# DeltaNet attention followed by a hierarchical gated mixture of experts: large element-wise work on VectorE instead of GpSimd, routing pushed at every third round, scatters declared independent, one Sqrt for the norms

## The chip, the cores and the metric

The kernel runs on one core of one Trainium2 chip. Its time is the device time of one execution in microseconds (us); the profile is one such execution taken by the hardware profiler. The engines are PE (TensorE matmul; PEld is its weight load), DVE (VectorE), ACT (ScalarE), POOL (GpSimd) and SP (SyncE, which here only issues DMAs). Each takes its own instructions strictly in order.

## The reference

Two stages follow each other. The first is a delta-rule recurrence over 768 tokens for 4 batches and 8 heads of width 48; the second sends each of the 3072 resulting rows (384 wide) to one of 16 experts.

```python
k_n = k / (np.linalg.norm(k, axis=-1, keepdims=True) + 1e-06)
for t in range(S):
    y[:, :, t] = einsum('bhd,bhde->bhe', q[:, :, t], state)
    v_old = einsum('bhde,bhd->bhe', state, k_n[:, :, t])
    state = state + beta_t * einsum('bhd,bhe->bhde', k_n[:, :, t], v[:, :, t] - v_old)
...
x = y.transpose(0, 2, 1, 3).reshape(B * S, H * D)
g_idx = argmax(x @ w_group); e_idx = argmax(x @ w_expert[g_idx])      # per token
out[token] = g_w * e_w * (relu(x @ w1[g, e]) @ w2[g, e])              # softmax weights of the two picks
```

## The kernel before

**Attention.** The 768 tokens are cut into NCH = 24 chunks of C = 32; the 4 batches fill the 128 partitions. Four chunks make a group (RG = 4), six groups in all. For a chunk u:

- `gram(u)` multiplies keys by keys and queries into the PSUM tile `g_ps` (one buffer, tag "g", which `t_ps`, `l_ps` and `r_ps` share). ScalarE copies the key half into `gt`, then the query half into `gq`; GpSimd masks `gq` (L173). Grams run LEAD = 9 chunks ahead.
- `inverse(g)` inverts the 32x32 triangular matrices of a group's 1024 (chunk, batch, head) problems. It is a generator, one or a few instructions a step: a transposition (L185), norms by Ln and Exp on ScalarE (L192, L193), the product `m`·`r` (L214) and the matrix `cs` (L216), each 128x1024, then 30 pairs of VectorE instructions (L224 multiply, L228 add, j = 1 to 30, 30 to 240 elements), the product with `cs` (L230), the diagonal (L231) and a transposition to `mt` (L235). Outside group 0, L214 and L230 run on GpSimd; L216 and L231 do always.
- `scale(u)` multiplies the values by the norms into `vh` on GpSimd (L241).
- `advance(u)` is the recurrence: PE `a_ps` from the state, VectorE `f` = `vh` - `a_ps` (L260), PE `w_ps` from `mt` and `f`, ScalarE `w`, PE `s_ps`, ScalarE state `s_bd` (two instructions, L290), and so to `a_ps` of the next chunk. PE `o_ps` gives the chunk's output, ScalarE copies it into `x` (ten buffers).

**Routing.** `logits(u)` transposes `x` on PE (`t_ps`), multiplies by the router weights (`l_ps`), and VectorE copies the result to `lg`. `route(r)` is a generator of some 28 small steps for a group of four chunks, mostly VectorE, with `pick`, `hot` and four `acc` on GpSimd, one matmul pair `r_ps` that counts tokens ahead of each token, `rk`, `slot`, `slot_i` on VectorE, and then four times a small copy (L410) and an indirect DMA (L413) from GpSimd that scatters 128 rows of `x` to the experts' places in `x_dram`. The scatters all write `x_dram`, which is first filled with zeros by 16 DMAs from SP (L495).

**Order.** Everything but SP's queue is issued in the order in which the Python code runs. The list `behind` holds the running generators; `work(n)` goes n rounds over it and pushes each one step, `route` only at every second round. `work` stands between the steps of `advance`, so VectorE's queue holds 19 rounds of inverse and route steps per chunk between one `f` and the next. A generator that yields ACT_STEP or PE_STEP is held until `allow`, once a chunk. SP's queue is put in order by the framework, by its own estimate.

**Experts.** After the last scatter SP reads the sorted rows (`xg`, L523) and 16 experts run one after the other (L538 to L557).

Of the kernel before, what the change touches and what calls it, by code (L numbers as in the profile page):

```python
# [52 lines left out]
def deltanet_then_moe(  # L53
# [57 lines left out]
    with ExitStack() as first:  # L111
# [35 lines left out]
        zero = ap_.tile([128, STATIC * XW], F32, name="zero")  # L147
        nc.gpsimd.memset(zero, 0.0)

        gts, gqs, mts, norm, vhs, xs = {}, {}, {}, {}, {}, {}  # L150

        def gram(u):


            g, uu = divmod(u, RG)
            kqt = kqt_[u % NB]
            if uu == 0:
                gts[g] = wk.tile([128, C, RG, H], F32, tag="gt", name=f"gt{g}")
            g_ps = ps.tile([128, 2, 512], F32, tag="g", name=f"g_ps{u}")
            g_out = g_ps[:, :, 0:NP * 2 * C].rearrange("p f (j a t) -> p f j a t", j=NP, a=2)  # L160
            for j in range(NP):
                for b in range(B):
                    for hh in range(2):
                        rows = slice(hh * 64, hh * 64 + D)
                        nc.tensor.matmul(g_out[quads[b], hh, j], lhsT=kqt[rows, 0, j, quads[b]],  # L165
                                         rhs=kqt[rows, :, j, quads[b]], start=True, stop=True,
                                         skip_group_check=True)
            nc.scalar.activation(
                gts[g][:, :, uu].rearrange("p t (f j) -> p f j t", f=2), g_out[:, :, :, 0, :],
                ACT.Copy)  # L170
            gq = wk.tile([128, 2, NP, C], F32, tag="gq", name=f"gq{u}", bufs=LEAD + 1)
            nc.scalar.activation(gq, g_out[:, :, :, 1, :], ACT.Copy)  # L172
            nc.gpsimd.tensor_tensor(  # L173
                gq, gq, cut["upper"][:, None, None, :].to_broadcast([128, 2, NP, C]),
                op=ALU.mult)
            gqs[u] = gq

        def inverse(g):

            eng = nc.gpsimd if g else nc.vector
            m = wk.tile([128, C, C], F32, tag="m", name=f"m{g}")
            flat = m.rearrange("p i j -> p (i j)")
            nc.vector.transpose(out=flat, in_=gts.pop(g).rearrange("p t u h -> p (t u h)"))  # L185
# [3 lines left out]
                           for n in ("nrm", "r0", "r1")]  # L189
            nc.vector.tensor_tensor(r0, diag, cut["tiny"].to_broadcast([128, C]), op=ALU.max)  # L190
            yield ACT_STEP
            nc.scalar.activation(r0, r0, ACT.Ln)  # L192
            nc.scalar.activation(r0, r0, ACT.Exp, scale=0.5)  # L193
            yield
            nc.vector.reciprocal(r1, r0)
            yield
# [14 lines left out]
            yield  # L211
            norm[g] = sm.tile([128, C], F32, tag="normt", name=f"normt{g}")
            nc.vector.transpose(out=norm[g], in_=nrm)
            eng.tensor_tensor(m, m, r0[:, :, None].to_broadcast([128, C, C]), op=ALU.mult)  # L214
            cs = wk.tile([128, C, C], F32, tag="cs", name=f"cs{g}")
            nc.gpsimd.tensor_tensor(cs, cut["below"].rearrange("p (i j) -> p i j", i=C),  # L216
                                    r0[:, None, :].to_broadcast([128, C, C]), op=ALU.mult)
            for _ in range(6 if g else 0):
                yield
            for j in range(1, C - 1):  # L220
                n = C - 1 - j
                t = wk.tile([128, C * C // 4], F32, tag="t", name=f"t{g}_{j}")
# [4 lines left out]
                yield  # L227
                nc.vector.tensor_tensor(m[:, j + 1:, 0:j], m[:, j + 1:, 0:j], tv, op=ALU.add)  # L228
                yield
            eng.tensor_tensor(m, m, cs, op=ALU.mult)  # L230
            nc.gpsimd.tensor_scalar(diag, r0, -1.0, None, op0=ALU.mult)  # L231
            for _ in range(6 if g else 0):
                yield
            mt = wk.tile([128, RG * H, C], F32, tag="mt", name=f"mt{g}")
            nc.vector.transpose(out=mt.rearrange("p r i -> p i r"), in_=flat)  # L235
            mts[g] = mt
# [1 line left out]
        def scale(u):  # L238
            g, uu = divmod(u, RG)
            vh = wk.tile([128, H, D], F32, tag="vh", name=f"vh{u}")  # L240
            nc.gpsimd.tensor_tensor(  # L241
                vh.rearrange("p (j f) d -> p f j d", f=2),
                kv_[u % NV][:, 1].rearrange("p (j f) d -> p f j d", f=2),
                norm[g][:, uu * H:(uu + 1) * H].rearrange("p (f j) -> p f j", f=2)[:, :, :, None]
                .to_broadcast([128, 2, NP, D]), op=ALU.mult)
            vhs[u] = vh
# [90 lines left out]
            yield  # L337
            return den

        lg_ = {}  # L340

        def logits(u):

# [17 lines left out]
        def route(r):  # L361
# [46 lines left out]
            for g, u in enumerate(us):  # L408
                x = xs.pop(u)
                nc.gpsimd.tensor_copy(x[:, DM:DM + 1], cw[:, g])  # L410
                for _ in range(2):
                    yield
                nc.gpsimd.indirect_dma_start(  # L413
                    out=x_dram.rearrange("t p d -> (t p) d"),
                    out_offset=bass.IndirectOffsetOnAxis(ap=slot_i[:, g], axis=0),
                    in_=x[:, :], in_offset=None)
                yield


# [11 lines left out]
        def work(n):  # L431

            for _ in range(n):
                rounds[0] += 1
                for task, pace in [(t, 2 if t.__name__ == "route" else 1) for t in behind]:
                    if held.get(task) is None and rounds[0] % pace == 0:
                        push(task)

# [9 lines left out]

        with tc.manual_schedule(engines={mybir.EngineType.PE, mybir.EngineType.DVE,
                                         mybir.EngineType.Activation, mybir.EngineType.Pool}):  # L450
            for u in range(RG):
                gram(u)
            behind.append(inverse(0))
            for step in range(LEAD - RG):
                work(2)
                allow(ACT_STEP)
                gram(RG + step)
            while behind:
                work(1)
            scale(0)  # L460
# [4 lines left out]
            for u in range(NCH + 1):  # L465
# [3 lines left out]
                next(turned)  # L469
                work(6)  # L470
                next(step)
                if u + LEAD < NCH:
                    gram(u + LEAD)
                work(6)
                next(step)
                next(turned)
                next(step)
# [180 lines left out]
```

## Time and profile before

| | us |
|---|---|
| median of 3 runs (722.49 to 725.14) | 722.54 |
| the profiled execution | 723.04 |
| its span, first to last instruction | 721.2 |
| PE busy, of the span | 555.5 |
| DVE busy | 248.4 |
| ACT busy | 150.5 |
| POOL busy | 158.4 |

The span lacks 1.84 us of the execution's own time (723.04 - 721.2), which lie around it. Busy time is the union of an engine's instructions; a matmul's end is modelled. In the text below, "first f" to "last f" are the L260 instructions of chunks 1 to 23, which start at 71.23 us (chunk 1), 113.85 (chunk 4), 293.05 (chunk 20) and 314.20 (chunk 23).

### The profile page before, as it was taken

Reading aid. Unit: us, or ns where it says so; the run is one execution under the profiler, and the core shown is the slowest. Engines: PE = TensorE matmul, PEld = TensorE weight load, DVE = VectorE, ACT = ScalarE, POOL = GpSimd, SP = SyncE. Lnnn points to the kernel's source line nnn. Section 1 sums busy time; section 2 is a strip of 40 time slices with the busy share of each in tenths; the row PEclk is TensorE's granted clock in tenths of the full one; section 3 lists DMA queues with packets and bytes.
Section 4 is the critical chain, followed back from the end, with each engine's and each line's share of the span. In section 5 each row is a group of like instructions: output and inputs, shape, how many; then the busy total and the mean of one; then the engine's idle time right before and its main releaser. Section 6 shows DMA issues by size and latency. Waiting matters only on the chain. (4 is left out here: it accounts for less than half of the span.)

```text
span 721.2 us, 20232 instructions
## 1 busy us (share of the span) xinstructions
PE 555.5 (77%) x9170; PEld 434.5 (60%) x9170; DVE 248.4 (34%) x703; ACT 150.5 (21%) x267; POOL 158.4 (22%) x222
## 2 busy tenths in 40 slices
PE   2304778667767677870399999999999999999994
PEld 2204667656656566750277766677766777667772
DVE  3787736855867668322101111000111001110100
ACT  2403324343343423320011100011000111001110
POOL 4313123344254353423100111010111001110001
PEclk9999656887677757885599999999999999999998
DMA  9904787223211121101225454454554554644200
GB/s 231 259 0 134 215 273 239 74 69 117 66 57 60 46 63 58 66 15 44 99 99 199 131 209 161 153 203 148 192 197 127 202 178 151 216 144 168 94 14 16
DMA packets 42374, 93.53 MB, mean 130 GB/s; under 512 B 3608, under 2 KB 28362, under 8 KB 42288
## 3 DMA queue, kind: packets, MB, share of 16 engines
q1 hardware_dynamic: 38704, 82.76, 35.9%
q0 software_dynamic: 3584, 9.47, 3.6%
q8 instruction: 72, 1.18, 0.7%
q14 instruction: 14, 0.11, 0.1%
HBM read 76.43 MB, written 17.36 MB: 130 GB/s over the span
## 5 line engine op out<-in xcount | busy, mean ns | idle before, releaser
L546 PE MATMUL h_ps<-xt,w 128*128 128x256 f32 x768 | 171.1, 383 | 8.1 <-DVE xt L540 8.1
L553 PE MATMUL y_ps<-w,hid 128*128 128x384 f32 x512 | 167.7, 486 | 0.0
L546 PEld LDWEIGHTS h_ps<-xt,w 128*128 128x128 f32 x768 | 145.4, 191 | 31.2 <-DVE xt L540 11.7
L553 PEld LDWEIGHTS y_ps<-w,hid 128*128 128x128 f32 x512 | 97.3, 190 | 64.4
L549 ACT ACTIVATE hid<-h_ps 128x512 f32<-128x512 f32 x64 | 38.2, 597 | 328.6 <-PE h_ps L546 328.6
L557 POOL DMA_INDIRECT out_dram<-yo,at x32 | 31.5, 983 | 331.7 <-DVE yo L556 327.5
L556 DVE TENSOR_SCALAR yo<-y_ps,xg 128x384 f32<-128x384 f32 x32 | 19.8, 618 | 225.6 <-PE y_ps L553 225.6
L224 DVE TENSOR_TENSOR t<-m 128x30 f32<-128x30 f32 (+9 forms) x180 | 80.8, 449 | 10.6 <-POOL m L214 7.7
L228 DVE TENSOR_TENSOR m<-m,t 128x30 f32<-128x30 f32 (+9 forms) x180 | 64.9, 361 | 5.6
L272 PE MATMUL w_ps<-f,mt 32*32 32x48 f32 x1472 | 27.5, 236 | 45.0 <-DVE f L260 43.2
L272 PEld LDWEIGHTS w_ps<-f,mt 32*32 32x32 f32 x1472 | 23.5, 130 | 50.7 <-DVE f L260 46.7
L165 PE MATMUL g_ps<-kqt 48*32 48x64 f32 x1536 | 28.3, 289 | 23.4 <-ACT gq L172 9.2
L290 ACT ACTIVATE s_bd<-s_ps 48x768 f32<-48x768 f32 x46 | 37.0, 805 | 29.5 <-PE s_ps L283 28.8
L283 PE MATMUL s_ps<-w,kv 32*48 32x48 f32 x1472 | 28.6, 248 | 17.3 <-issue 11.7
L528 DVE TENSOR_SCALAR at<-xg 128x2 int32<-128x2 f32 x16 | 2.7, 168 | 109.2 <-DMA xg<-x_dram 109.2
L165 PEld LDWEIGHTS g_ps<-kqt 48*32 48x32 f32 x1536 | 21.9, 138 | 27.8 <-issue 12.9
L283 PEld LDWEIGHTS s_ps<-w,kv 32*48 32x48 f32 x1472 | 24.1, 152 | 21.8 <-issue 14.0
L413 POOL DMA_INDIRECT x_dram<-x,slot_i x24 | 24.7, 1030 | 56.2 <-DMA x_dram<-x,slot_i 42.9
L294 PE MATMUL o_ps<-w,gq 32*32 32x48 f32 x1536 | 31.7, 246 | 3.0 <-issue 2.9
L256 PE MATMUL a_ps<-s_bd,kqt 128*32 128x96 f32 x736 | 29.6, 322 | 4.2 <-issue 3.4
L173 POOL TENSOR_TENSOR gq<-gq,con 128x256 f32<-128x256 f32 x24 | 18.3, 764 | 61.7 <-ACT gq L172 61.7
L294 PEld LDWEIGHTS o_ps<-w,gq 32*32 32x32 f32 x1536 | 26.7, 137 | 4.9 <-issue 3.9
(95 smaller groups left out, 455.8 us busy)
## 6 DMA issues: line engine op xcount, KB each, us to landing
w<-in_w_dram SPq DMA_DIRECT2D x32, 1536.0 KB, 7.2
kqt<-in_kq_dram SPq DMA_DIRECT2D x48, 192.0 KB, 6.1
kv<-in_kv_dram SPq DMA_DIRECT2D x24, 384.0 KB, 3.3
x_dram<-zero SPq DMA_DIRECT2D x16, 386.0 KB, 7.7
xg<-x_dram SPq DMA_DIRECT2D x16, 386.0 KB, 7.7
con<-in_const_dram SPq DMA_DIRECT2D x1, 754.0 KB, 6.3
out_dram<-yo,at POOLq DMA_INDIRECT x32, 4.0
x_dram<-x,slot_i POOLq DMA_INDIRECT x24, 3.0
```

The costliest lines, as they stand in the source:

```text
L165: nc.tensor.matmul(g_out[quads[b], hh, j], lhsT=kqt[rows, 0, j, quads[b]], rhs=kqt[rows, :, j, quads[b]], start=True, stop=True, skip_grou ...
L224: nc.vector.tensor_tensor(tv, m[:, j + 1:, j:j + 1].to_broadcast([128, n, j]), m[:, j:j + 1, 0:j].to_broadcast([128, n, j]), op=ALU.mult)
L228: nc.vector.tensor_tensor(m[:, j + 1:, 0:j], m[:, j + 1:, 0:j], tv, op=ALU.add)
L256: nc.tensor.matmul(a_ps[quads[b], 2 * j:2 * j + 2, :], lhsT=kqt[:, 0, j, quads[b]], rhs=s_bd[:, b, j], start=True, stop=True, skip_group_c ...
L272: nc.tensor.matmul(w_ps[b, h], lhsT=mt[b, uu * H + (h % 2) * NP + h // 2], rhs=f[b, h], start=True, stop=True, skip_group_check=True)
L283: nc.tensor.matmul(s_at[hh * 64:hh * 64 + D, b, j], lhsT=k[quads[b], 2 * j + hh], rhs=w[quads[b], 2 * j + hh], start=(u == 0 and j == 0), ...
L290: nc.scalar.activation(s_bd[rows, :, :, hh, :], s_at[rows], ACT.Copy)
L294: nc.tensor.matmul(o_ps[b, h], lhsT=gq[b, h % 2, h // 2], rhs=w[b, h], start=(u == 0 and h == 0), stop=True, skip_group_check=True)
L546: nc.tensor.matmul(h_ps[:, k], lhsT=w1[:, j, (f + k) * 128:(f + k + 1) * 128], rhs=xt[:, j], start=(j == 0), stop=(j == DC - 1), skip_grou ...
L549: nc.scalar.activation(hid[:, f:f + 2], h_ps, ACT.Relu)
L553: nc.tensor.matmul(y_ps, lhsT=hid[:, f, i * 128:(i + 1) * 128], rhs=w2[:, f], start=(f == 0), stop=(f == FC - 1))
L557: nc.gpsimd.indirect_dma_start(out=out[:, :], out_offset=bass.IndirectOffsetOnAxis(ap=at[:, i:i + 1], axis=0), in_=yo[:, :], in_offset=Non ...
```

## The change

Six edits:

1. The mask of `gq` moves to VectorE and reads `g_ps` itself; ScalarE's copy of the query half is gone. `gram` returns the mask as a function, which is called at once in the opening and after `work(4)` in the loop.
2. `m`·`r`, `cs`, `m`·`cs`, the diagonal and `vh` move to VectorE. The six idle steps on either side of the 30 pairs are replaced by one step for each moved instruction.
3. Ln and Exp(0.5 x) become one Sqrt; one Sqrt on a constant stands at the head of ScalarE's queue.
4. `route` is pushed at every third round instead of every second.
5. A chunk has 20 rounds (6 + 4 + 3 + 7) instead of 19 (6 + 6 + 7).
6. The scatters are declared free of each other.

```diff
-            nc.scalar.activation(gq, g_out[:, :, :, 1, :], ACT.Copy)
-            nc.gpsimd.tensor_tensor(
-                gq, gq, cut["upper"][:, None, None, :].to_broadcast([128, 2, NP, C]),
-                op=ALU.mult)
             gqs[u] = gq
+            return lambda: nc.vector.tensor_tensor(
+                gq, g_out[:, :, :, 1, :],
+                cut["upper"][:, None, None, :].to_broadcast([128, 2, NP, C]), op=ALU.mult)
...
-            nc.scalar.activation(r0, r0, ACT.Ln)
-            nc.scalar.activation(r0, r0, ACT.Exp, scale=0.5)
+            nc.scalar.activation(r0, r0, ACT.Sqrt)
...
-            eng.tensor_tensor(m, m, r0[:, :, None].to_broadcast([128, C, C]), op=ALU.mult)
+            yield
+            nc.vector.tensor_tensor(m, m, r0[:, :, None].to_broadcast([128, C, C]), op=ALU.mult)
+            yield
             cs = wk.tile([128, C, C], F32, tag="cs", name=f"cs{g}")
-            nc.gpsimd.tensor_tensor(cs, cut["below"].rearrange("p (i j) -> p i j", i=C),
+            nc.vector.tensor_tensor(cs, cut["below"].rearrange("p (i j) -> p i j", i=C),
                                     r0[:, None, :].to_broadcast([128, C, C]), op=ALU.mult)
-            for _ in range(6 if g else 0):
-                yield
+            yield
...
-            eng.tensor_tensor(m, m, cs, op=ALU.mult)
-            nc.gpsimd.tensor_scalar(diag, r0, -1.0, None, op0=ALU.mult)
-            for _ in range(6 if g else 0):
-                yield
+            nc.vector.tensor_tensor(m, m, cs, op=ALU.mult)
+            yield
+            nc.vector.tensor_scalar(diag, r0, -1.0, None, op0=ALU.mult)
+            yield
...
-            nc.gpsimd.tensor_tensor(
+            nc.vector.tensor_tensor(
                 vh.rearrange("p (j f) d -> p f j d", f=2),
...
-                nc.gpsimd.indirect_dma_start(
+                put = nc.gpsimd.indirect_dma_start(
...
-                    in_=x[:, :], in_offset=None)
+                    in_=x[:, :], in_offset=None).ins
+                if puts:
+                    tc.declare_no_dep(put, group="puts", reason="a token's slot is its own")
+                tc.add_to_no_dep_group("puts", put)
+                puts.append(put)
...
-                for task, pace in [(t, 2 if t.__name__ == "route" else 1) for t in behind]:
+                for task, pace in [(t, 3 if t.__name__ == "route" else 1) for t in behind]:
...
+            nc.scalar.activation(rooted, cut["tiny"], ACT.Sqrt)
...
-                if u + LEAD < NCH:
-                    gram(u + LEAD)
-                work(6)
+                masks = gram(u + LEAD) if u + LEAD < NCH else lambda: None
+                work(4)
+                masks()
+                work(3)
```

VectorE's queue in the opening, before: the end of the norms of group 0 (`r`, `nrm`), `m`·`r` (L214) and the first of the 30 pairs.

```order
L201 SCALAR_TENSOR_TENSOR nrm_303<-r_304,con 128x32
L205 RECIPROCAL r_305<-nrm_303 128x32
L207 TENSOR_TENSOR r_305<-r_305 128x32
L209 SCALAR_TENSOR_TENSOR r_304<-r_305,bt 128x32
L213 STREAM_TRANSPOSE normt_465<-nrm_303 128x32
L214 TENSOR_TENSOR m_301<-m_301,r_304 128x1024
L224 TENSOR_TENSOR t_1_470<-m_301 128x30
```

The same place now; the `gq` rows are the masks of chunks 6, 7 and 8, each reading that chunk's `g_ps`.

```order
L174 TENSOR_TENSOR gq_417<-g_ps_383,con 128x256
L203 RECIPROCAL r_303<-nrm_301 128x32
L205 TENSOR_TENSOR r_303<-r_303 128x32
L174 TENSOR_TENSOR gq_455<-g_ps_421,con 128x256
L207 SCALAR_TENSOR_TENSOR r_302<-r_303,bt 128x32
L211 STREAM_TRANSPOSE normt_458<-nrm_301 128x32
L174 TENSOR_TENSOR gq_495<-g_ps_461,con 128x256
L213 TENSOR_TENSOR m_299<-m_299,r_302 128x1024
L216 TENSOR_TENSOR cs_498<-con,r_302 128x1024
L223 TENSOR_TENSOR t_1_500<-m_299 128x30
```

`m`·`r` of group 0 now stands behind the mask of the ninth gram, and `cs` behind `m`·`r`.

SP's queue around the zero fill (`x_dram<-zero`), with `kqt` and `kv` the chunks' inputs and `w` the experts' weights; + is the change.

```order
 L127 DMA kqt_87<-in_kq_dram 48x1024 x2
-L495 DMA x_dram<-zero 128x2x386 x3
+L500 DMA x_dram<-zero 128x2x386 x15
 L132 DMA kv_99<-in_kv_dram 128x768
-L495 DMA x_dram<-zero 128x2x386 x2
+L500 DMA x_dram<-zero 128x2x386
+L105 DMA w_0_1254<-in_w_dram 128x3x1024
 L127 DMA kqt_88<-in_kq_dram 48x1024 x2
-L495 DMA x_dram<-zero 128x2x386 x2
+L106 DMA w_0_1255<-in_w_dram 128x8x384
 L132 DMA kv_100<-in_kv_dram 128x768
-L495 DMA x_dram<-zero 128x2x386 x9
```

Fifteen of the sixteen zero fills moved ahead of the first `kv` of the loop, and the first two experts' weights moved up one to two chunks.

GpSimd's queue at the end of routing, before: the scatters of the last group but one, then `pick`, `hot` and `acc` of the last group.

```order
L410 COPY x_4436<-cw 128x1
L413 DMA x_dram<-x_4436,slot_i 49152x386
L410 COPY x_4636<-cw 128x1
L413 DMA x_dram<-x_4636,slot_i 49152x386
L410 COPY x_4836<-cw 128x1
L413 DMA x_dram<-x_4836,slot_i 49152x386
L410 COPY x_5026<-cw 128x1
L413 DMA x_dram<-x_5026,slot_i 49152x386
L371 TENSOR_TENSOR pick<-lg,gh 128x64
L382 TENSOR_TENSOR hot<-gh,eh 128x64
L387 TENSOR_TENSOR acc<-acc,hot 128x16 x4
L410 COPY x_5196<-cw 128x1
```

And now:

```order
L409 COPY x_4390<-cw 128x1
L412 DMA x_dram<-x_4390,slot_i 49152x386
L409 COPY x_4594<-cw 128x1
L412 DMA x_dram<-x_4594,slot_i 49152x386
L409 COPY x_4794<-cw 128x1
L370 TENSOR_TENSOR pick<-lg,gh 128x64
L412 DMA x_dram<-x_4794,slot_i 49152x386
L409 COPY x_4989<-cw 128x1
L412 DMA x_dram<-x_4989,slot_i 49152x386
L381 TENSOR_TENSOR hot<-gh,eh 128x64
L386 TENSOR_TENSOR acc<-acc,hot 128x16 x4
L409 COPY x_5154<-cw 128x1
```

`pick` moved ahead of two of the four scatters; `hot` still stands behind all four. None of these scatters waits for the one before it any more.

## Rows read from the trace of the kernel before

**Rows 1.** Windows: stage, its length, busy us of each engine, granted clock, DMA share, GB/s.

```profile
71.20:113.80 42.60, 29.36 (x987) 25.82 (x987) 23.19 (x59) 14.63 (x25) 7.90 (x11) 0.62 0.82 258
113.80:293.00 179.20, 133.04 (x4960) 116.91 (x4960) 126.10 (x396) 67.61 (x122) 77.24 (x109) 0.73 0.26 75
207.60:219.10 11.50, 10.36 (x329) 9.21 (x329) 7.55 (x17) 3.42 (x6) 8.55 (x9) 0.50 0.22 73
314.20:352.10 37.90, 7.64 (x188) 6.29 (x188) 6.79 (x39) 2.40 (x6) 10.88 (x22) 0.61 0.12 43
352.10:721.20 369.10, 347.97 (x1376) 254.81 (x1376) 37.43 (x80) 38.22 (x64) 31.46 (x32) 0.98 0.44 150
```

**Rows 2.** Waits of DVE from 113 to 293: total us, times, longest us.

```profile
DVE f L260 <- POOL vh L241: 10.5, 3, 4.4
DVE lg L358 <- PE l_ps L356: 9.9, 6, 2.2
DVE r L195 <- ACT r L193: 7.9, 3, 2.7
DVE rk L401 <- PE r_ps L398: 7.3, 4, 2.3
DVE t L224 <- POOL m L214: 5.8, 4, 1.4
DVE sel L375 <- POOL pick L371: 5.2, 3, 2.9
```

**Rows 3.** Groups by line, whole span: busy us, mean ns, idle before.

```profile
L224 DVE TENSOR_TENSOR t<-m 128x30 f32<-128x30 f32 (+9 forms) x180 | 80.8, 449 | 10.6 <-POOL m L214 7.7
L228 DVE TENSOR_TENSOR m<-m,t 128x30 f32<-128x30 f32 (+9 forms) x180 | 64.9, 361 | 5.6
L260 DVE TENSOR_TENSOR f<-vh,a_ps 128x384 f32<-128x384 f32 x23 | 12.6, 550 | 17.2 <-POOL vh L241 10.5 <-PE a_ps L256 6.7
L413 POOL DMA_INDIRECT x_dram<-x,slot_i x24 | 24.7, 1030 | 56.2 <-DMA x_dram<-x,slot_i 42.9 <-ACT xt L352 5.5 <-PE o_ps L294 3.0
```

**Rows 4.** Timeline of the opening: start us, us, instruction, idle before it.

```profile
24.50 1.21 DVE L214 TENSOR_TENSOR m<-m,r 128x1024 f32<-128x1024 f32 x1
...
33.36 1.18 PE L165 MATMUL g_ps<-kqt 48*32 48x64 f32 x64 [0.91 <-ACT gq L172]
...
34.22 2.52 POOL L216 TENSOR_TENSOR cs<-con,r 128x1024 f32<-128x1024 f32 x1
34.53 2.46 DVE L224 TENSOR_TENSOR t<-m 128x228 f32<-128x228 f32 x1
...
43.15 0.40 DVE L224 TENSOR_TENSOR t<-m 128x228 f32<-128x228 f32 x1
...
51.24 0.19 DVE L228 TENSOR_TENSOR m<-m,t 128x30 f32<-128x30 f32 x1
...
55.27 1.50 PE L272 MATMUL w_ps<-vh,mt 32*32 32x48 f32 x64 [20.73 <-DVE mt L235]
```

**Rows 5.** Timeline: PE's longest pause without a releaser between 76 and 114.

```profile
88.34 1.18 PE L283 MATMUL s_ps<-w,kv 32*48 32x48 f32 x58 [4.08 <-issue]
```

**Rows 6.** Timeline of the end of routing.

```profile
321.05 1.02 POOL L413 DMA_INDIRECT x_dram<-x,slot_i  x1 [5.55 <-ACT xt L352]
...
321.91 0.18 DVE L358 COPY lg<-l_ps 128x20 f32<-128x20 f32 x1 [1.73 <-PE l_ps L356]
...
324.61 0.97 POOL L413 DMA_INDIRECT x_dram<-x,slot_i  x1 [2.34 <-DMA x_dram<-x,slot_i]
...
332.77 0.30 POOL L371 TENSOR_TENSOR pick<-lg,gh 128x64 f32<-128x64 f32 x1
...
338.34 1.03 POOL L413 DMA_INDIRECT x_dram<-x,slot_i  x1 [2.16 <-DVE over L511]
...
352.06 1.40 SPq L523 DMA_DIRECT2D xg<-x_dram  x3
```

More of the change, by code (lines that the diff above doesn't have):

```diff
@@ L148, in deltanet_then_moe @@
         nc.gpsimd.memset(zero, 0.0)
+        rooted = sm.tile([128, 1], F32, tag="rooted", name="rooted", bufs=1)
         gts, gqs, mts, norm, vhs, xs = {}, {}, {}, {}, {}, {}
@@ L171, in gram @@
             gq = wk.tile([128, 2, NP, C], F32, tag="gq", name=f"gq{u}", bufs=LEAD + 1)
-            nc.scalar.activation(gq, g_out[:, :, :, 1, :], ACT.Copy)
-            nc.gpsimd.tensor_tensor(
-                gq, gq, cut["upper"][:, None, None, :].to_broadcast([128, 2, NP, C]),
-                op=ALU.mult)
             gqs[u] = gq
+            return lambda: nc.vector.tensor_tensor(
+                gq, g_out[:, :, :, 1, :],
+                cut["upper"][:, None, None, :].to_broadcast([128, 2, NP, C]), op=ALU.mult)
         def inverse(g):
-            eng = nc.gpsimd if g else nc.vector
             m = wk.tile([128, C, C], F32, tag="m", name=f"m{g}")
@@ L338, in total @@
             return den
-        lg_ = {}
+        lg_, puts = {}, []
         def logits(u):
@@ L450, in deltanet_then_moe @@
                                          mybir.EngineType.Activation, mybir.EngineType.Pool}):
+            nc.scalar.activation(rooted, cut["tiny"], ACT.Sqrt)
             for u in range(RG):
-                gram(u)
+                gram(u)()
             behind.append(inverse(0))
@@ L456, in deltanet_then_moe @@
                 allow(ACT_STEP)
-                gram(RG + step)
+                gram(RG + step)()
             while behind:
```

## The prediction, made before the changed kernel had run

> **What bounds the kernel now.** I read the windows by stage first. From 352.1 us the experts keep PE busy 347.97 of 369.1 us at a granted clock of 0.98 [rows 1]; the change does not touch them, so all that it can win lies in the 352 us before. Those I cut at the `f` instructions: the opening to the first f at 71.2; B, chunks 1 to 4, 42.6 us; C, chunks 4 to 20, 179.2 us, where an inverse always runs; D, chunks 20 to 23, 21.2 us; E, from the last f to the first read of the sorted rows, 37.9 us [rows 1].
>
> In C no engine is full: PE 133.0, VectorE 126.1, GpSimd 77.2, ScalarE 67.6 of 179.2 [rows 1]. The queue that sets the pace is VectorE's, since every `f` stands behind some 19 rounds of inverse and route steps: 179.2 us are 126.1 of work and 53.1 of standing still. The list of its waits says for whom: 21.5 for GpSimd (`vh` 10.5, `m`·`r` 5.8, `pick` 5.2), 17.2 for `l_ps` and `r_ps` on PE, 7.9 for the norms on ScalarE [rows 2].
>
> Part of its 126.1 is hidden waiting as well. The 30 pairs of an inverse, undisturbed: from j = 19 (43.15) to the end of j = 30 (51.43) twelve pairs take 8.28 us; j = 1 to 12 have the same sizes; the six between take 0.40 + 0.04 an instruction, 5.3; together 21.9, of which 60 gaps of 0.04 are 2.4, so 19.5 busy [rows 4]. Six inverses would be 117 us; the two lines show 80.8 + 64.9 = 145.7 [rows 3]. So 28.7 us were lost inside instructions. Where, one row shows: 228 elements that take 0.40 at 43.15 take 2.46 at 34.53, from just after GpSimd began `cs` (2.52 us) until that ended [rows 4]. Four of the six inverses run in C, which by share is 19 of the 28.7; adding its instructions against their undisturbed durations gives 17, which I take. The Trainium skill ("SBUF — State Buffer", section "SBUF: two separate sides") says that VectorE and GpSimd share a port pair under an exclusive lock, held for a whole instruction; the trace agrees, with the 2.46 us.
>
> In E the chain is visible instruction by instruction: scatters come 3.56 us apart (321.05, 324.61), each after the landing of the one before, `pick` stands behind four of them at 332.77 although `lg` was there at 321.91, and four more run from 338.34 to the read at 352.06 [rows 6].
>
> **The change part by part.**
>
> *Opening: +5.* `m`·`r` ran at 24.50 while the grams went on until 34.54 (33.36 + 1.18) [rows 4]. Now it stands behind nine masks, the last of which needs the ninth gram. ScalarE's second copy no longer holds the bank, which I put at 0.3 us a gram, eight times: the ninth gram ends near 32.1, its mask at 32.6 (I take 0.45 for 256 elements, from 0.40 at 228 and 0.55 at 384 [rows 3, 4]). Then `m`·`r` 1.25, `cs` 1.25 (as long as `m`·`r`'s 1.21 and a gap), the pairs 21.9, `m`·`cs` 1.25, diagonal 0.25, transposition 1.95, `vh` 0.6: `w_ps` at 61.0 against 55.27 [rows 4], +5.8. Up to the first f the second inverse is rid of GpSimd's lock and has `cs`, a mask and a `vh` more on VectorE: -0.8. Bounds: +3 if PE's pauses shrink, +8 if fifteen zero fills, now issued there, lengthen them.
>
> *B: -8.* VectorE works 23.2 of 42.6 and stands 19.4 [rows 1]. DMA share is 0.82 here and PE pauses up to 4.08 us without a releaser [rows 5]; most zero fills leave this stretch and the weights spread out, and the wait for GpSimd's `m`·`cs` goes. I halve the standing to 9.5. Work: -2.5 of lock, + `m`·`cs` 1.2, diagonal 0.2, three `vh` 1.65, three masks 1.35: 25.1. Sum 34.6. Bounds -14 (little standing left) to -2 (pauses stay).
>
> *C: -14.* Work: 126.1 - 17 of lock. Added for four inverses 4 x (3 x 1.21 + 0.2) = 15.3, for 16 `vh` 8.8 (0.55 as `f`, also 384 elements [rows 3]), for 11 masks 5.0; I take 1.5 off because independent neighbours overlap: 136.7. Standing: 53.1 less the 21.5 for GpSimd, whose queue is left with small instructions and scatters that wait for nothing, less 4 because VectorE comes later to `lg` and `rk`: 27.6. Sum 164.3 against 179.2, of which I book 14. The Sqrt I cost at nothing: ScalarE is busy 67.6 of 179.2 [rows 1]; without that cover it would shorten the 7.9 for the norms, a gain. The slower pace of `route` adds no instruction; its scatters come later, which costs only if `x` (ten buffers) runs out. Bounds: standing down to 15, -27; `vh` and `pick` waits refilled by others, no overlap, +6.
>
> *D: -1* (-2 to +1): no inverse runs there, PE and ScalarE hold the chain.
>
> *E: -12.7.* On the old clock: in PE's queue `r_ps` of the last group but one now follows the last `l_ps`, so `lg` comes at about 321.0, and `rk`, `slot`, `slot_i` until 322.7; the first scatter, with 0.9 allowed for its start, 323.6. A scatter is 1.03 on GpSimd [rows 3] plus a copy of 0.2: 1.25 apart if none waits. `pick` after the second: 326.0. From `pick` to the first scatter of the last group was 5.57 (332.77 to 338.34 [rows 6]); two scatters now stand in between, of which VectorE's steps hide all but 1.0: 332.6. Three more at 1.25, then 3.04 to landing (352.06 - 338.34 - 3 x 3.56 [rows 6]): 339.4 against 352.06. Bounds: 1.25 apart exactly -14; still 3.56 apart -2.
>
> Sum: +5 - 8 - 14 - 1 - 12.7 = -30.7 on the profiled execution's 723.04, so 692.3; that execution is 0.5 above the median of the runs, so **692**.
>
> **The rivals.**
>
> *PE's clock.* In one chunk of C, with VectorE late, PE ran at 0.50 and was busy 10.36 of 11.5 us [rows 1]: at the lower of its two levels a chunk's matmuls alone fill it. In C the granted clock is 0.73 [rows 1]. If PE idles before each `f` and stays low, C is 16 x 11.2 = 179, no gain: 723 - 30.7 + 14, **706**. For it: the longer VectorE queue keeps `f` late. Against it: PE stood still after VectorE's waits on GpSimd, which go. The Trainium skill ("TensorE: Matmul & The Clock Gate", Part 1) has the clock fall to half after idling and return with sustained work; by that rule shorter stalls help and evenly late `f` hurts, and the 0.50 in that chunk agrees.
>
> *Scatters still one after the other*, as GpSimd's queue or the DMA ring may hold them: E only -2, **703**. Against it: the wait shown is for the landing of the earlier write, 42.9 us in all [rows 3].
>
> *More waits vanish.* VectorE comes late enough that `lg`, `rk` and the norms are always there: standing in C 15, **679**.
>
> *The mask holds the bank: slower.* `g_ps` has one buffer. It was freed by ScalarE right after the gram; now by a mask ten rounds down VectorE's queue, and `l_ps`, `o_ps` and `a_ps` queue behind that on PE. A set of PE instructions takes about 1.4 in the slow chunk (10.36 over seven to eight sets [rows 1]). VectorE would stand 1.8 at `lg` and about 1 at `f`, 2.8 a chunk in 15 masked chunks, 42 less the 6 kept for `lg`: +36, **728**. It decides against the change from about 2.4 us a masked chunk. Against it: ten rounds are some 4.5 us, and the gram and `s_ps` take PE nearly as long.
>
> **How the numbers follow.** Forecast 0.61, clock 0.15, scatters chained 0.06, more waits vanish 0.13, bank held 0.05. The range of eight in ten takes in the better case's side and the clock case, not the slow one: 676 to 707. About 0.5% (3.6 us) is what can be told from no change. All cases but the last are faster by more; I leave 0.03 for mixtures near zero: faster 0.92, same 0.03, slower 0.05.
>
> **What the profile after would show.** `w_ps` of chunk 0 near 61 us with `m`·`r` behind the ninth mask; L224 and L228 near 117 us in all; no wait of VectorE for GpSimd's `vh`; about 45 fewer us waited for `x_dram` landings on GpSimd; scatters about 1.25 apart in E and the read some 25 us after the last f; C near 165 us with VectorE busy about 137. I am wrong if C stays at 179 with a clock below 0.7, if scatters stay 3.5 apart, or if `l_ps` waits for the mask.

## The result, and the profile after

The changed kernel takes 697.88 us (median of 4 runs, 695.84 to 699.90), the kernel before 722.51 beside it (4 runs, 720.15 to 725.14): a ratio of 0.9658, 95% interval 0.9614 to 0.9702. The profiled execution took 697.92 us against 723.04.

The windows of the changed kernel, cut at its own `f` instructions of chunks 1, 4, 20 and 23 and at the first read of the sorted rows, answer to [rows 1]:

```profile
core 0: us, PE busy (x) PEld busy (x) DVE busy (x) ACT busy (x) POOL busy (x), PEclk, DMA share, GB/s
76.50:114.60 38.10, 25.84 (x984) 22.71 (x984) 23.28 (x63) 10.72 (x18) 0.00 (x0) 0.72 0.61 189
114.60:274.30 159.70, 124.78 (x4944) 109.48 (x4940) 133.62 (x432) 66.92 (x109) 24.89 (x59) 0.80 0.25 77
274.30:300.50 26.20, 22.31 (x807) 19.41 (x799) 5.88 (x24) 9.36 (x16) 6.93 (x16) 0.79 0.12 42
300.50:326.90 26.40, 8.38 (x188) 6.80 (x180) 7.94 (x47) 2.50 (x7) 12.17 (x28) 0.63 0.17 61
326.90:696.10 369.20, 347.42 (x1376) 254.47 (x1376) 37.39 (x80) 38.22 (x64) 31.46 (x32) 0.98 0.44 150
```

D in the kernel before, for comparison:

```profile
293.10:314.20 21.10, 17.02 (x760) 14.57 (x760) 4.79 (x23) 9.34 (x17) 8.03 (x20) 0.92 0.12 42
```

The opening is 5.3 us longer (76.5 against 71.2), B 4.5 shorter, C 19.5 shorter, D 5.0 longer, E 11.5 shorter, and the experts are as before: together 25.2, the whole difference. In C VectorE works 133.6 us, 7.5 more than before, and stands 26.1 instead of 53.1.

The list of VectorE's waits in C (from 114.6 to 274.3 us) answers to [rows 2]; the waits for `vh`, `t` and `pick` are gone:

```profile
DVE r L193 <- ACT r L191: 7.8, 3, 3.0
DVE rk L400 <- PE r_ps L397: 5.4, 3, 2.3
DVE lg L357 <- PE l_ps L355: 4.9, 6, 1.2
DVE f L259 <- PE a_ps L255: 0.9, 2, 0.6
```

The groups by line of the changed kernel: the pairs of the inverse take 118.8 us in all, where [rows 3] had 145.7; the third row shows PE waiting 10.4 us for the mask before `l_ps`:

```profile
L227 DVE TENSOR_TENSOR m<-m,t 128x30 f32<-128x30 f32 (+9 forms) x180 | 59.5, 330 | 4.5
L223 DVE TENSOR_TENSOR t<-m 128x30 f32<-128x30 f32 (+9 forms) x180 | 59.3, 330 | 4.6
...
L355 PE MATMUL l_ps<-wr,xt 128*128 128x20 f32 x144 | 25.0, 304 | 15.7 <-DVE gq L174 10.4 <-issue 4.6 <-ACT xt L351 0.6
```

The timeline in the opening, around the ninth gram. PE waits 1.15 us for the mask of the gram before it, where it waited 0.91 for ScalarE's second copy [rows 4]. The ninth mask waits for ScalarE's `gt`, which reads the same PSUM tile, and `m`·`r` starts at 34.67 behind it instead of at 24.50 [rows 4]:

```profile
32.42 1.18 PE L166 MATMUL g_ps<-kqt 48*32 48x64 f32 x64 [1.15 <-DVE gq L174]
33.70 0.60 ACT L169 ACTIVATE gt<-g_ps 128x256 f32<-128x256 f32 x1 [1.79 <-PE g_ps L166]
34.33 0.42 DVE L174 TENSOR_TENSOR gq<-g_ps,con 128x256 f32<-128x256 f32 x1 [1.75 <-ACT gt L169]
34.67 1.21 DVE L213 TENSOR_TENSOR m<-m,r 128x1024 f32<-128x1024 f32 x1
35.80 1.22 DVE L216 TENSOR_TENSOR cs<-con,r 128x1024 f32<-128x1024 f32 x1
```

GpSimd's timeline at the end of routing answers to [rows 6]. The scatters no longer wait for a landing, come 1.44 to 1.58 us apart, and `pick` stands behind two of them:

```profile
310.35 1.02 POOL L412 DMA_INDIRECT x_dram<-x,slot_i  x1 [3.44 <-DVE gt L315]
...
311.85 0.97 POOL L412 DMA_INDIRECT x_dram<-x,slot_i  x1 [0.28 <-POOL x L409]
312.82 0.19 POOL L409 COPY x<-cw 128x1 f32<-128x1 f32 x1
312.97 0.30 POOL L370 TENSOR_TENSOR pick<-lg,gh 128x64 f32<-128x64 f32 x1
313.43 1.03 POOL L412 DMA_INDIRECT x_dram<-x,slot_i  x1 [0.17 <-POOL pick L370]
...
324.06 0.97 POOL L412 DMA_INDIRECT x_dram<-x,slot_i  x1 [0.28 <-POOL x L409]
```

### The profile page after: what moved, and what is told of

Read it like the earlier page. It is cut to its first block, busy times and chain, and to the rows that moved or that the text cites. A ratio compares the mean times of both kernels' runs of the same rounds, so it can differ in the third digit from the quotient of the medians.

```text
span 696.1 us, 20147 instructions
## 1 busy us (share of the span) xinstructions
PE 549.5 (79%) x9170; PEld 429.6 (62%) x9170; DVE 260.0 (37%) x773; ACT 138.6 (20%) x233; POOL 82.9 (12%) x152
## 3 DMA queue, kind: packets, MB, share of 16 engines
q8 instruction: 72, 1.18, 0.7%
## 5 line engine op out<-in xcount | busy, mean ns | idle before, releaser
L558 PE MATMUL y_ps<-w,hid 128*128 128x384 f32 x512 | 167.7, 486 | 0.0
L554 ACT ACTIVATE hid<-h_ps 128x512 f32<-128x512 f32 x64 | 38.2, 597 | 322.9 <-PE h_ps L551 322.9
L227 DVE TENSOR_TENSOR m<-m,t 128x30 f32<-128x30 f32 (+9 forms) x180 | 59.5, 330 | 4.5
L223 DVE TENSOR_TENSOR t<-m 128x30 f32<-128x30 f32 (+9 forms) x180 | 59.3, 330 | 4.6
L166 PE MATMUL g_ps<-kqt 48*32 48x64 f32 x1536 | 26.8, 271 | 22.4 <-issue 9.9
L282 PE MATMUL s_ps<-w,kv 32*48 32x48 f32 x1472 | 25.9, 227 | 17.1 <-issue 12.3
L355 PE MATMUL l_ps<-wr,xt 128*128 128x20 f32 x144 | 25.0, 304 | 15.7 <-DVE gq L174 10.4
L271 PE MATMUL w_ps<-f,mt 32*32 32x48 f32 x1472 | 23.1, 213 | 15.9 <-DVE f L259 15.3
L282 PEld LDWEIGHTS s_ps<-w,kv 32*48 32x48 f32 x1472 | 21.7, 134 | 21.2 <-issue 14.2
L255 PE MATMUL a_ps<-s_bd,kqt 128*32 128x96 f32 x736 | 31.9, 337 | 2.5 <-issue 1.7
L355 PEld LDWEIGHTS l_ps<-wr,xt 128*128 128x128 f32 x144 | 22.3, 231 | 18.2 <-DVE gq L174 11.8
L271 PEld LDWEIGHTS w_ps<-f,mt 32*32 32x32 f32 x1472 | 19.5, 112 | 21.5 <-DVE f L259 17.9
```

What stands on the lines that cost most here:

```text
L223: nc.vector.tensor_tensor(tv, m[:, j + 1:, j:j + 1].to_broadcast([128, n, j]), m[:, j:j + 1, 0:j].to_broadcast([128, n, j]), op=ALU.mult)
L255: nc.tensor.matmul(a_ps[quads[b], 2 * j:2 * j + 2, :], lhsT=kqt[:, 0, j, quads[b]], rhs=s_bd[:, b, j], start=True, stop=True, skip_group_c ...
L271: nc.tensor.matmul(w_ps[b, h], lhsT=mt[b, uu * H + (h % 2) * NP + h // 2], rhs=f[b, h], start=True, stop=True, skip_group_check=True)
L282: nc.tensor.matmul(s_at[hh * 64:hh * 64 + D, b, j], lhsT=k[quads[b], 2 * j + hh], rhs=w[quads[b], 2 * j + hh], start=(u == 0 and j == 0), ...
L355: nc.tensor.matmul(l_ps, lhsT=xt[:, j], rhs=wr[:, j], start=(j == 0), stop=(j == DC - 1))
L554: nc.scalar.activation(hid[:, f:f + 2], h_ps, ACT.Relu)
```

## The experiments

Twelve kernels ran, four at a time beside the kernel before, each four on a chip of their own. The kernel before took 725.15 us there beside numbers 1 to 4, 727.48 beside 5 to 8 and 724.19 beside 9 to 12; a ratio is taken from all runs of the two kernels and is not the quotient of the two medians. The table has each one's ratio and the stages of its profiled execution, cut at the starts of the same instructions. The first three columns of stages end at the `f` of chunks 1, 4 and 20, D at the last `f`, E at the first read of the sorted rows.

| kernel | median us | ratio, 95% interval | opening | B | C | D | E |
|---|---|---|---|---|---|---|---|
| before | 722.51 | 1 | 71.2 | 42.6 | 179.2 | 21.1 | 37.9 |
| changed | 697.88 | 0.9658 (0.9614 to 0.9702) | 76.5 | 38.1 | 159.7 | 26.2 | 26.4 |
| 1 before + scatters | 704.53 | 0.9740 (0.9680 to 0.9799) | 71.6 | 42.1 | 168.1 | 23.6 | 25.0 |
| 2 changed, chained | 715.48 | 0.9857 (0.9791 to 0.9922) | 78.1 | 39.0 | 161.9 | 25.2 | 38.9 |
| 3 changed, late masks | 699.38 | 0.9641 (0.9596 to 0.9686) | 68.0 | 36.0 | 174.5 | 23.9 | 27.4 |
| 4 changed, pace 2 | 699.07 | 0.9650 (0.9596 to 0.9704) | 76.2 | 37.6 | 156.3 | 26.5 | 25.7 |
| 5 changed, Ln and Exp | 713.96 | 0.9855 (0.9800 to 0.9910) | 78.2 | 38.1 | 172.1 | 23.7 | 27.6 |
| 6 changed, `vh` on GpSimd | 704.48 | 0.9725 (0.9667 to 0.9784) | 78.6 | 33.5 | 168.4 | 22.8 | 27.5 |
| 7 changed, inverse on GpSimd | 710.06 | 0.9780 (0.9724 to 0.9836) | 76.9 | 37.6 | 170.7 | 25.8 | 29.4 |
| 8 changed, loads (a repeat) | 703.40 | 0.9702 (0.9644 to 0.9759) | 76.5 | 38.2 | 165.0 | 24.8 | 27.3 |
| 9 before + Sqrt | 720.04 | 0.9914 (0.9878 to 0.9949) | 70.6 | 42.1 | 177.1 | 22.5 | 38.0 |
| 10 changed, masks on GpSimd | 695.67 | 0.9600 (0.9566 to 0.9634) | 68.7 | 40.1 | 163.3 | 25.4 | 27.3 |
| 11 changed, waits hidden | 694.74 | 0.9573 (0.9536 to 0.9610) | 79.1 | 36.6 | 155.9 | 26.0 | 26.7 |
| 12 before + scatters + Sqrt | 699.96 | 0.9662 (0.9619 to 0.9705) | 68.5 | 40.7 | 167.7 | 24.6 | 25.2 |

Number 8 turned out to be the changed kernel once more (below). Its C is 5.3 us longer than that of the changed kernel with the same order of instructions, so a difference of some 5 us in C between two profiles says nothing by itself. Numbers 5 to 7 ran on its chip and are compared with it; the others are compared with the changed kernel by their ratios.

**1. The scatters alone.** The kernel before with edit 6:

```diff
+                if puts:
+                    tc.declare_no_dep(put, group="puts", reason="a token's slot is its own")
+                tc.add_to_no_dep_group("puts", put)
+                puts.append(put)
```

> The kernel before with one part of the change: the scatters declared independent. Theory (the end is a term of its own, worth 11.5 us, and needs no other part): from the last f to the read of the sorted rows about 26 us against 37.9, scatters about 1.5 us apart there, and in the middle part VectorE's waits for pick (5.2) mostly gone and some of those for vh (10.5), whose GpSimd queue no longer stands still at landings: 704 us (698 to 711). Rival (independence is of use only once GpSimd is rid of its large work): at the end, where no large work is left, the same gain, but in the middle nothing, 711. Second rival (the scatters are held by the queue all the same and the shorter end came from the moved work): 720 or more.

Measured 704.53, E 25.0 and C 168.1. The head of VectorE's waits in C (113.7 to 281.9 us) has neither `vh` nor `pick` any more, though both still run on GpSimd:

```profile
DVE lg L358 <- PE l_ps L356: 11.8, 8, 2.4
DVE rk L401 <- PE r_ps L398: 7.5, 4, 3.0
DVE r L195 <- ACT r L193: 7.4, 3, 2.7
DVE t L224 <- POOL m L214: 5.8, 4, 1.4
```

So `vh` was not late because GpSimd is slow at it, but because it stood in GpSimd's queue behind scatters that waited for landings. One edit of five lines gives most of the 25 us: 2.6% by the ratio, 20.6 us by the medians (704.53 against 725.15 beside it). In the profiled execution C is 11.1 us shorter and E 12.9, while D is 2.5 longer. The wait for `m`·`r` (5.8) stays.

**2. The other edits without it.** The changed kernel without those five lines.

> The changed kernel with the scatters waiting for one another again. Theory: the end is back at about 38 us, +11.5; in the middle VectorE waits for pick again, some 4 us: 713 us (709 to 717). Rival (GpSimd has so little left that a chained scatter delays nobody): the end alone partly longer, 704. If the scatters come 3.5 us apart at the end and the middle part keeps its 160 us, the two terms are independent of each other.

Measured 715.48, as the theory had it. At the end the scatters are 3.4 to 3.8 us apart again, as GpSimd's timeline shows:

```profile
314.01 1.02 POOL L412 DMA_INDIRECT x_dram<-x,slot_i  x1 [3.96 <-DVE gt L315]
...
317.77 0.97 POOL L412 DMA_INDIRECT x_dram<-x,slot_i  x1 [2.53 <-DMA x_dram<-x,slot_i]
...
321.41 1.02 POOL L412 DMA_INDIRECT x_dram<-x,slot_i  x1 [2.22 <-ACT ex L326]
```

E is 12.5 longer, C only 2.2, and VectorE does not wait for `pick` in C, where the theory had some 4 us of it. So much of what edit 6 gains in C and what the other five edits gain there are the same microseconds: either takes them. That it is the move of `vh` among the five is likely, but was not tried by itself with the scatters chained.

**3. The first nine masks later.** ScalarE copies the query half out of PSUM for chunks 0 to 8, and VectorE masks it in SBUF behind the first inverse:

```diff
+            if u < LEAD:
+                nc.scalar.activation(gq, g_out[:, :, :, 1, :], ACT.Copy)
+                return lambda: nc.vector.tensor_tensor(
+                    gq, gq, cut["upper"][:, None, None, :].to_broadcast([128, 2, NP, C]),
+                    op=ALU.mult)
...
-                gram(RG + step)()
+                later.append(gram(RG + step))
```

> The changed kernel; of the first nine grams ScalarE copies the second half out of PSUM as before, and VectorE masks it in SBUF after the first inverse. Theory (the opening's +5 comes from the first inverse's m times r standing behind the ninth mask): m times r back near 24.5 us, w_ps of chunk 0 near 53 against 62.7, the nine masks (some 4 us) then stand ahead of the first f, which comes 6 us earlier, near 70.5; total 692 us (689 to 695). Rival (PE's pauses and the zero fills set the first f): w_ps earlier, first f still near 75, total 697.

`m`·`r` at 23.89, `w_ps` at 51.95 and the first `f` at 68.05 came as expected, the `f` of chunk 4 10.6 earlier. The total did not: 699.38. C took all of it back, in the same order of instructions. Its window:

```profile
104.00:278.50 174.50, 136.96 (x4936) 118.70 (x4936) 134.39 (x433) 67.07 (x109) 25.64 (x63) 0.73 0.29 86
```

VectorE works as long as in the changed kernel (134.4 against 133.6), PE 12.2 longer for the same matmuls, at a mean granted clock of 0.73 instead of 0.80. PE's waits in that window also have more pauses without a releaser, 18.5 us in these four rows against 10.6 in the changed kernel, and VectorE waits 17.4 us for PE at `lg` and `f` instead of 5.8:

```profile
PE s_ps L287 <- issue: 7.3, 5, 2.5
...
PE g_ps L166 <- issue: 5.1, 7, 2.7
PE o_ps L298 <- issue: 3.8, 6, 1.5
...
PE w_ps L276 <- issue: 2.3, 4, 1.0
```

The theory holds for the opening and fails for the time; the rival named the wrong place. What made PE slower there was not tried by itself.

**4. Routing at every second round.** The 3 in `work` is a 2 again.

> The changed kernel with routing again paced at every second round. Theory (pace adds no instruction and is close to free): the middle part shorter or longer by up to 2 us, total 698 (695 to 701). Rival (the pace of three, which holds a routing step back into the last chunks, is what lengthened chunks 20 to 23 from 21.2 to 26.2 us): these back near 22, total 693. Second rival (the pace of three is what gave the middle part more than forecast): the middle part back near 165, total 703.

Measured 699.07, no difference; D stays at 26.5, so the pace does not explain D. (The profiled execution, 693.3 us, is the shortest of runs that reach 703.3.) In C VectorE's wait for the norms is 1.6 us here instead of 7.8, and its wait at `lg` 9.0 instead of 4.9: the one went, most of it came back at the other, and the median did not move.

**5. Ln and Exp again.** The Sqrt at the head of ScalarE's queue is left out as well.

```diff
-            nc.scalar.activation(r0, r0, ACT.Sqrt)
+            nc.scalar.activation(r0, r0, ACT.Ln)
+            nc.scalar.activation(r0, r0, ACT.Exp, scale=0.5)
```

> The changed kernel with the norms by Ln and Exp again instead of one Sqrt. Theory (ScalarE has cover, so the Sqrt costs and gives nothing): more table loads of 1.283 us, VectorE's wait for the norms (7.8 us in the middle part) longer by up to 3 us, ratio to the kernel before 0.966 to 0.972 (about 700). Rival (each group's norm stands on the path): one more load and one more activation for each of six groups, about 9 us, ratio 0.978.

Measured 713.96 against the repeat's 703.40: 10.6 us or 1.5%, the rival's size. ScalarE's timeline in one group shows two table loads between VectorE's `r` and its norm, 3.0 us:

```profile
154.94 1.28 ACT L191 ACT_TABLE_LOAD   x1
156.24 0.23 ACT L191 ACTIVATE r<-r 128x32 f32<-128x32 f32 x1
156.49 1.28 ACT L192 ACT_TABLE_LOAD   x1
157.78 0.23 ACT L192 ACTIVATE r<-r 128x32 f32<-128x32 f32 x1
```

In the changed kernel, the same place: one load and the Sqrt, 1.5 us. The table for Exp comes back ten us earlier, with routing, where VectorE has other work:

```profile
141.11 1.28 ACT L326 ACT_TABLE_LOAD   x1
...
151.49 1.28 ACT L191 ACT_TABLE_LOAD   x1
152.79 0.23 ACT L191 ACTIVATE r<-r 128x32 f32<-128x32 f32 x1
```

VectorE's wait for the norms in C is 12.4 us instead of the repeat's 6.7, which is 5.7 of the 7.1 by which C is longer (172.1 against 165.0). PE's clock in C is 0.75 instead of the repeat's 0.79; what that adds was not tried by itself. The Trainium skill ("ScalarE: Activation LUTs", section "Table sets: the hidden batching unit") has Ln followed by Exp as one load from a common table. Here each of the two is preceded by a load of its own, six before Ln and six before Exp, of 1.283 us each, and the measurement decides.

**6. `vh` on GpSimd again.** In `scale`, `nc.vector` is `nc.gpsimd` again.

> The changed kernel with the vh product on GpSimd again. Theory from the run with the scatters alone (VectorE waited 10.5 us for vh only because vh stood behind chained scatters in GpSimd's queue): no wait for vh to speak of, VectorE's work in the middle part 8 us shorter, part of that given back because a GpSimd instruction on SBUF holds VectorE up; ratio 0.960 to 0.967. Rival (vh on GpSimd comes late or holds VectorE up for more than the 0.55 us that it saves): waits of f for vh of 5 us or more, ratio 0.975.

Measured 704.48 against 703.40: no difference. The wait for `vh` is 1.7 us, once. Neither range was hit: VectorE's work in C is only 2.5 shorter (131.57 against 134.07) and not 8. Its instructions take longer again: over the whole span the line of the additions takes 62.6 us against 59.5, that of the products 60.0 against 59.4, and `cs` 8.6 against 7.3.

**7. The inverse's large products on GpSimd again.** `m`·`r`, `cs`, `m`·`cs` and the diagonal with the idle rounds of before:

```diff
-            nc.vector.tensor_tensor(m, m, r0[:, :, None].to_broadcast([128, C, C]), op=ALU.mult)
-            yield
+            eng.tensor_tensor(m, m, r0[:, :, None].to_broadcast([128, C, C]), op=ALU.mult)
...
-            yield
+            for _ in range(6 if g else 0):
+                yield
```

> The changed kernel with the inverse's three large products and its diagonal on GpSimd again, with the waiting rounds of before. Theory (these moves take away time lost inside VectorE's instructions, some 28 us in six inverses, and put 22 us of work in its place, so that the middle part gains little): the two lines of pairs back from 119 to about 145 us, the middle part 163 to 168 against 160, ratio 0.970 to 0.978. Rival (the moves are where the gain of the middle part comes from): middle part 175, ratio 0.987.

Measured 710.06 against 703.40, 6.7 us or 0.9% longer; the two intervals overlap a little. The ratio, 0.978, is at the theory's edge, and C, 170.7, lies between the two. Only one of the two lines of pairs grows, by 11 us and not 26:

```profile
L223 DVE TENSOR_TENSOR t<-m 128x30 f32<-128x30 f32 (+9 forms) x180 | 70.2, 390 | 9.1 <-POOL m L213 4.8
L227 DVE TENSOR_TENSOR m<-m,t 128x30 f32<-128x30 f32 (+9 forms) x180 | 59.5, 331 | 4.6
```

Of the 26.9 us by which the two lines were longer in the kernel before (145.7 against 118.8), 10.9 come back here, 3.8 with `vh` on GpSimd (number 6) and 5.8 with the masks there (number 10, lines of 64.0 and 60.6). The remaining 6.4 no run shows by itself.

**8. Weights later.** `if u in (2, 3)` became `if u in (9, 10)` for the first two experts' loads.

> The changed kernel with the first two experts' weights fetched at chunks 9 and 10 instead of 2 and 3. Theory (PE's pauses without a releaser, 8.4 us from 90 to 120, come where the weights are on their way): chunks 1 to 4 shorter by 4 us or more, chunks 9 to 12 longer by about as much, total the same, ratio 0.960 to 0.970. Rival (the pauses belong to the code at that place): chunks 1 to 4 stay at 38 us with the same pauses, and nothing changes at chunks 9 to 12.

SP's queue is the one whose order the code does not set, and it came out as it was: the loads start between 69.25 and 101.84 us (68.67 to 101.79 in the changed kernel). The run does not try its theory and is a repeat of the changed kernel: 703.40 on this chip, ratio 0.9702. (What the traces say of these pauses stands below, under B.) Its C:

```profile
114.80:279.80 165.00, 129.07 (x4950) 111.49 (x4952) 134.07 (x433) 66.78 (x109) 26.31 (x63) 0.79 0.26 74
```

**9. The Sqrt alone.** The kernel before with edit 3.

> The kernel before with one Sqrt for the norms instead of Ln and Exp, nothing else. Theory (each group's norm stands on VectorE's path, also before: undone in the changed kernel it cost 1.9%): VectorE's wait for the norms from 7.9 to about 4 us, the middle part 4 to 12 us shorter than 179, ratio 0.983 to 0.994. Rival (in the kernel before, waits for GpSimd end later and swallow it): ratio 0.995 or more.

Measured 720.04, ratio 0.9914, as the theory had it. C is only 2.1 us shorter and not 4 to 12: the wait for the norms falls from 7.9 to 2.2 us, but that at `lg` grows from 9.9 to 14.4 and that at `rk` from 7.3 to 9.7. Two of its rows, from 113 us:

```profile
DVE lg L358 <- PE l_ps L356: 14.4, 8, 3.2
DVE r L195 <- ACT r L193: 2.2, 3, 1.1
```

**10. All masks as before.** ScalarE's copy and GpSimd's mask (edit 1 undone).

> The changed kernel with every mask as before: ScalarE copies the second half of the gram, GpSimd masks it in SBUF. Theory (the mask on VectorE costs the opening 5 us and saves ScalarE and GpSimd work that nobody waits for; the opening's gain is mostly given back later, as in the run with late masks): first f near 71, the middle part a few us longer than 160, ratio 0.960 to 0.972. Rival (the mask on VectorE is a part that pays): ratio 0.978 or more, with PE waiting longer for the copies of ScalarE.

Measured 695.67, ratio 0.9600: not slower than the changed kernel, and perhaps faster (the intervals overlap a little). The first `f` is 7.8 us earlier, C 3.6 longer, which is within what two profiles of one program differ by. In C PE's wait for the mask before `l_ps` is gone; for ScalarE's copy it waits 0.2 us there. The mask on VectorE buys nothing.

**11. Waits hidden.** Rounds between a releaser and the instruction that needs it:

```diff
             nc.scalar.activation(r0, r0, ACT.Sqrt)
-            yield
+            for _ in range(8 if g > 1 else 1):
+                yield
...
+            for _ in range(1):
+                yield
             rk = small("rk", [NE])
```

> The changed kernel with eight empty rounds behind the Sqrt and one behind the r_ps matmuls, so that other VectorE instructions stand between each wait's releaser and the instruction that needs it. Theory (VectorE's standing is what is left of the middle part): the waits for the norms (9.3 us) and for r_ps (8.4 us) mostly gone, half of that seen in the time, ratio 0.953 to 0.960. Rival (PE at its lower clock is as long as VectorE by now): the waits go over to a_ps and l_ps, ratio 0.963 to 0.970.

Measured 694.74, ratio 0.9573, the fastest of all; its interval lies below those of the changed kernel (just) and of its repeat, which ran on another chip; it overlaps that of number 10. VectorE's waits in C (115.7 to 271.6), and the window:

```profile
DVE lg L358 <- PE l_ps L356: 6.0, 6, 2.2
DVE f L260 <- PE a_ps L256: 4.9, 3, 2.3
DVE rk L403 <- PE r_ps L398: 3.1, 3, 1.8
DVE gq L174 <- ACT gt L169: 2.5, 4, 0.9
DVE r L194 <- ACT r L191: 0.6, 1, 0.6
```

```profile
115.70:271.60 155.90, 123.38 (x4964) 106.24 (x4960) 134.85 (x439) 67.07 (x109) 29.36 (x63) 0.83 0.27 80
```

Of the norms' 7.8 all but 0.6 are gone, and 2.3 of `rk`'s 5.4; 4.0 came back at `a_ps`, 1.1 at `l_ps` and 2.5 at `gq`. The time is what the theory said; the waits moved in part as the rival said.

**12. Scatters and Sqrt, nothing moved.** The kernel before with edits 3 and 6.

> The kernel before with the scatters independent and one Sqrt, none of the moves from GpSimd to VectorE. Theory (these two alone are worth 2.6% and some 1.5%, and the moves mainly change where VectorE's time goes): ratio 0.955 to 0.967, as fast as the changed kernel. Rival (the Sqrt pays only once VectorE waits for GpSimd no more): ratio 0.970 to 0.976, as with the scatters alone, and the moves are worth the difference.

Measured 699.96, ratio 0.9662 against the changed kernel's 0.9658. Within the intervals the same gain comes without edits 1, 2, 4 and 5. In C VectorE works less and stands more than in the changed kernel:

```profile
109.20:276.90 167.70, 130.74 (x4969) 113.17 (x4962) 127.03 (x396) 69.29 (x120) 78.04 (x109) 0.78 0.29 87
```

## Why the prediction was right, and where not

The total of 692 came out at 697.9, 0.8% above and within the range, and "faster" was right. That it came so close is partly luck: C gave 5.5 us more than the sum had booked, while the opening, B, D and E together gave 11.0 less. By its own steps:

- **Opening, +5: measured +5.3, by other parts.** The chain it named is there, and number 3 confirms it: with `m`·`r` at 23.89 the first `f` comes 8.4 earlier. But "ScalarE's second copy no longer holds the bank, which I put at 0.3 us a gram" has the wrong sign: each mask waits for ScalarE's `gt`, which reads the same tile, and PE then waits 1.15 us for the mask instead of 0.91 for the copy. The ninth gram ends at 33.60 (32.42 + 1.18) instead of 32.1, its mask starts at 34.33, and `w_ps` at 62.72 instead of 61.0.
- **B, -8: measured -4.5.** The step that failed is "I halve the standing": VectorE stood 14.8 us instead of 9.5, after 19.4 before. The DMA share did fall, 0.82 to 0.61, but PE's pauses without a releaser stayed: between the first and the fourth `f` those of over 0.6 us add up to 10.6 us (2.27, 2.36, 1.35, 4.65), against 9.8 before (0.65, 4.08, 2.39, 1.15, 1.5). The largest in the changed kernel:

```profile
109.42 1.25 PE L355 MATMUL l_ps<-wr,xt 128*128 128x20 f32 x5 [4.65 <-issue]
```

Number 8, which should have told what they come from, did not move a transfer. The traces point at PE's own instructions. Every kernel's page has a queue for them, in the changed kernel:

```profile
q8 instruction: 72, 1.18, 0.7%
```

That is 72 packets of 16.4 KB. PE has 2 x 9170 matmuls and weight loads, so a packet holds some 255 instructions, or 128 matmuls with their loads, and that is the distance at which the pauses stand (last section). By the packets' times in the fourteen traces, all 175 pauses of over 0.6 us between 76 and 320 us end 1.2 to 1.7 us after such a packet has landed. The one above ends 1.4 us after a packet that started at 106.98, 2.2 us after PE had stopped, in a stretch where the DMA share is above 0.9 (104.7 to 109.5). No run changed this on purpose: that the packet was late there because the DMA engines were full is likely, but not shown.
- **C, -14: measured -19.5.** The terms of the sum were close: work 133.6 against 136.7, standing 26.1 against 27.6, and the pairs 118.8 against 117. Their sum, 164.3, was rounded down to a gain of 14; the repeat's C of 165.0 would have met it, so the rest is within what two profiles differ by. The reasons were only half right. The prediction took the 21.5 us of waits for GpSimd as one, to go with its large work and its chained scatters together. Number 1 shows that the chain alone held `vh` (10.5) and `pick` (5.2), so that large work held VectorE for the 5.8 at `m`·`r` alone, and that edit 6 by itself, in the kernel before, takes 11 us off C. The moves gain nothing on the whole: from number 12 to the changed kernel edits 1, 2, 4 and 5 give 8.0 in C and 2.6 in B and take 8.0 in the opening, 1.6 in D and 1.2 in E. They take away time lost inside instructions but put work in its place: in C VectorE works 133.6 us instead of 127.0.
- **"The Sqrt I cost at nothing": the step that failed most.** It is worth 0.9% in the kernel before (number 9) and 1.5% in the changed one (number 5). It is a gain that the sum lacks, so the other terms were too hopeful by as much more. The argument looked at how busy ScalarE is (67.6 of 179.2); but VectorE stands at the norms until ScalarE is through with them and with what is queued ahead of them, and little work of VectorE is queued between. Number 11, which puts some there, gains again. How the time follows from this wait is shown only in part: in number 9 the wait falls by 5.7 us and C by 2.1, and in number 4 it falls by 6.2 and the median not at all, since other waits for PE grow.
- **D, -1: measured +5.0.** The sign was wrong. PE holds the chain there, as the prediction said, but it is busy 22.3 us instead of 17.0, at a granted clock of 0.79 instead of 0.92 and with 807 matmuls in the stage instead of 760. The other kernels have 22.5 to 26.5 us there; the pace is not the cause (number 4). What lowers the clock there stays open.
- **E, -12.7: measured -11.5.** Right in mechanism; a scatter takes 1.44 to 1.58 us in the queue instead of 1.25, mostly because 0.28 us pass between the small copy and the scatter that takes it.

Of the rivals, the mask holding the bank exists, with 10.4 us of PE's waits, and "if `l_ps` waits for the mask" was one of the prediction's signs of being wrong. But little hung on it: VectorE's wait at `lg` fell all the same (9.9 to 4.9 in C), and number 10 takes the wait away and gains 0.6 points of ratio, with intervals that overlap. The clock was given as a case beside the forecast. It rather varies from run to run together with C, by up to 15 us with VectorE's order of instructions in C unchanged (numbers 3, 8 and the changed kernel: C 174.5, 165.0 and 159.7 at 0.73, 0.79 and 0.80, PE busy 137.0, 129.1 and 124.8). Which of the two follows the other is not shown, and number 6 has a C of 168.4 at 0.80.

Undone one at a time, the scatters cost 2.0 points of ratio, the Sqrt 1.5 and the inverse 0.8; alone the first two give 2.6 and 0.9, and together (number 12) 3.4. With intervals of some 0.4 to 0.6 points on either side, that is no sign that the parts help or hinder each other.

## What to carry to other kernels

A wait for an engine's result may be a wait for what stands ahead of it in that engine's queue: look first for a DMA there that waits for another DMA's landing, and free that, before moving work. Cover for an activation is not how idle ScalarE is but what the waiting engine has queued between asking and using: a few rounds of other work there took 0.9 to 1.3 points of ratio (number 11 against the changed kernel and its repeat), where the moves as a whole gave none (number 12). But add up the other waits too, since one that goes can come back at another engine (numbers 4 and 9). And before trusting a stage's difference between two profiles, see how far it differs between two executions of one program: here 5 us of 160.

## What the runs showed of the hardware

- At the end of routing, indirect scatters that do not wait for one another leave GpSimd 1.44 to 1.58 us apart, each 0.97 to 1.03 us long; chained they are 3.4 to 3.8 apart (the kernel before and number 2).
- PE's pauses without a releaser come at regular places of its instruction stream: in the kernel before those at 82.44, 88.34, 94.74, 100.93 and 105.14 us lie 127 to 130 matmuls apart, and in the changed kernel the three at 93.32, 98.15 and 109.42 lie 128 and 255 apart. In all fourteen kernels one of 1.8 to 3.1 us stands some 2390 to 2440 matmuls into the stream, at 124 to 133 us. Those of over 0.6 us add up to 23.9 us before the experts in the kernel before and 27 to 40 in the others, so that a few us between two profiles may be theirs alone. They end 1.2 to 1.7 us after a packet of the instruction queue has landed (under B above).
- GpSimd takes 1.91 us for `m`·`r`, 2.57 for `cs` and 2.35 for `m`·`cs` (number 7), VectorE 1.2 for each (the changed kernel).
- The Sqrt starts 0.02 us after its table load of 1.283 us ends (they start at 152.79 and 151.49).
